# Weighted values: the shared key chunk as two half-column products instead of one full product

## The chip, the cores and the metric

One core of a Trainium2 chip runs the whole program. The metric is the device time in microseconds of one execution. Before the change the median of three runs is 1622.12 us (1620.75 to 1624.53).

## What is computed

Attention that keeps the 32 largest scores of each row, for 8 batches and 8 heads of 576 tokens with 64 features, followed by a gated feed-forward layer over all 4608 tokens. The reference, cut to what matters:

```python
scores = scale * np.matmul(q, k.transpose(0, 1, 3, 2))
kth = np.partition(scores, -top_k, axis=-1)[..., -top_k:-top_k + 1]
scores = np.where(scores >= kth, scores, -1000000000.0)
attn = np.exp(scores - np.max(scores, axis=-1, keepdims=True))
attn = attn / (np.sum(attn, axis=-1, keepdims=True) + 1e-09)
attn_out = np.matmul(attn, v)                      # the change is here
...
gate = 1.0 / (1.0 + np.exp(-(x @ w_gate)))
out = (gate * (x @ w_val)) @ w_out
```

## The kernel before, in words

Heads are worked on in pairs, tokens in tiles of 128 (P), with a last tile of 64 (REM). For each batch, group of tiles and head pair, `run` goes through four stages that overlap over neighbouring steps. `scores` (L219, TensorE) makes the scores of both heads; `select` and `masked` (DVE, ACT, POOL) find each row's threshold and leave the masked exponentials `e`; `turn` (L321, L326, L329) transposes `e` on TensorE so that keys lie on the partitions (`et`, nine chunks of 128 keys, evicted by ACT at L322); `weigh` multiplies by the values.

The nine chunks of `et` hold the keys of two heads laid end to end: chunks 0 to 3 are of the first head, 5 to 8 of the second, and chunk 4 holds the last 64 keys of the first and the first 64 of the second. In `weigh`, for one or two tiles of 128 queries (n = 128 or 256 columns), L340 multiplies a 128x64 block of values of the second head into the upper half of the PSUM tile `po` and L341 one of the first head into the lower half, four times. L342 then multiplies chunk 4 by `mixed`, the blocks 4 and 5 of the value tile side by side (128x128). Block 4 is zero where chunk 4 holds keys of the second head, and block 5 where it holds keys of the first, so one product serves both halves. The last tile of 64 queries goes through L345 to L348, which the change leaves alone.

After the products, L351 transposes `inv`, the inverse row sums, on TensorE into the same PSUM bank (one transpose for each tile of 128 queries); ACT copies it out (`rs`, L354), DVE multiplies (`xf`, L357), ACT and POOL split the result (`xh` L364, `xl` L365), and the feed-forward layer (L396 to L398, L415 to L417, with the weights loaded by L382) consumes it. The value tile comes by one DMA a head pair (L177), with three buffers; `po` has one.

The order of the instructions on each engine isn't written out by hand. The program gives them in the order of `run`, with a rule that holds the feed-forward work behind the attention by a fixed number of tokens (`goal`), and the tile framework's scheduler then sets each engine's order from priorities and its own model of the time (`schedule_with_timeline_sim=True`). So TensorE's instructions from the feed-forward layer, the scores and the transposes are mixed, and a score product can stand in the middle of a `weigh`. All operands of `weigh` are float32, and the hardware makes each float32 product in two passes: every product line shows twice as many matmuls in the trace as the program has. The feed-forward products and the scores of all batches but the first work on a split into two parts (float32r).

Of the kernel before, what the change touches and what calls it, by code (L numbers as in the profile page):

```python
# [28 lines left out]
def tile_topk_attention_then_gated_ffn(  # L29
# [8 lines left out]
    nc = tc.nc  # L38
    P = 128
    B, H, _, S = k.shape  # L40
    D = P // 2
# [290 lines left out]
    def weigh(et, vt, n, invs, pieces, nm):  # L332

        both = ps_o.tile([P, 4 * P], F32, tag="o", name=f"po_{nm}")
        po, rb = both[:, :n], both[:, 2 * P :]
        if n > REM:
            mixed = vt[:, 4:6].rearrange("p a d -> p (a d)")

            for c in reversed(range(4)):
                nc.tensor.matmul(po[D:], vt[:, 6 + c], et[:, 5 + c, :n], start=c == 3, stop=False)  # L340
                nc.tensor.matmul(po[:D], vt[:, c], et[:, c, :n], start=c == 3, stop=False)  # L341
            nc.tensor.matmul(po, mixed, et[:, 4, :n], start=False, stop=True)  # L342
        else:
            for c in range(4):
                nc.tensor.matmul(po[:D], vt[:, c], et[:, c, :REM], start=c == 0, stop=False)  # L345
                nc.tensor.matmul(po[D:], vt[:, 6 + c], et[:, c, REM:P], start=c == 0, stop=False)
            nc.tensor.matmul(po[:D], vt[:REM, 4], et[:REM, 4, :REM], start=False, stop=True)
            nc.tensor.matmul(po[D:], vt[:REM, 10], et[:REM, 4, REM:P], start=False, stop=True)  # L348

        for t, inv in enumerate(invs):  # L350
            nc.tensor.transpose(rb[:, t * P : (t + 1) * P], inv, ident)  # L351
        rs = b2.tile([P, 2 * P], F32, tag="rs", name=f"rs_{nm}")
        m = len(invs) * P
        nc.scalar.activation(rs[:, :m], rb[:, :m], AF.Copy)  # L354
        xf = b2.tile([P, 2 * P], F32, tag="xf", name=f"xf_{nm}")[:, :n]
        if n > REM:
            nc.vector.tensor_tensor(xf, po, rs[:, :n], op=ALU.mult)  # L357
        else:
            for h in range(2):
                d = slice(h * D, h * D + D)  # L360
                nc.vector.tensor_tensor(xf[d], po[d], rs[d, h * REM : h * REM + REM], op=ALU.mult)
        o = 0
        for (xh, xl), c, k in pieces:
            nc.scalar.activation(xh[:, c : c + k], xf[:, o : o + k], AF.Copy)  # L364
            nc.gpsimd.tensor_tensor(xl[:, c : c + k], xf[:, o : o + k], xh[:, c : c + k], op=ALU.subtract)  # L365
            o += k
# [61 lines left out]
    def run(general):  # L428
# [32 lines left out]
        for n in range(len(steps) + 2):  # L461
# [42 lines left out]
            if len(invs) == 2 or i >= end - 1 or i == NT - 1:  # L504

                t, left, pieces = b * S + (i + 1 - len(invs)) * P, o, []
                while left:
                    u, c = t // U, t % U
                    if (u, p) not in xs:
                        if u % 3 == 2 and len(bxs) == 1:  # L510

                            for _ in todo.pop(0) if todo else ():
                                pass
                            split_done()
                        xs[u, p] = [bxs[u % 3 // 2].tile([P, U], F32R, tag=k, name=f"{k}{mark}_{u}_{p}") for k in ("xh", "xl")]
                    k = min(left, U - c)
                    pieces.append((xs[u, p], c, k))
                    t, left = t + k, left - k
                weigh(et, values[g, p], o, invs, pieces, nm)
# [77 lines left out]
```

## Time and profile before

| | |
|---|---|
| median of three runs | 1622.12 us (1620.75 to 1624.53) |
| the profiled execution, its own time | 1619.79 us |
| its span, from the first to the last instruction | 1618.0 us |
| mean granted TensorE clock | 0.981 |
| busy: PE / weight load / DVE / ACT / POOL | 1553.3 / 1391.1 / 1265.3 / 1168.9 / 1206.8 us |

How to read it: PE is TensorE's matmuls, whose shown durations overlap each other because they are pipelined, so the distance between two starts is what one of them takes from its engine. PEld is TensorE's load of the stationary operand, which can run beside the matmul before it. A row `x2` of the timeline merges two neighbours. 1.79 us of the profiled execution's own time lie outside its span.

### The profile page before, as it was taken

The page shows a single profiled execution, that of the slowest core. Times are in us where ns is not written, and L with a number is a line of the kernel's source. Part 1 is how long each engine was busy: PE and PEld are TensorE (multiplying, and loading weights), DVE is VectorE, ACT ScalarE, POOL GpSimd, SP SyncE. Part 2 cuts the span into 40 slices and gives each one's busy share as a digit, 9 for nine tenths or more (in the row PEclk, how much of TensorE's full clock was granted, in tenths as well). Part 3 has the DMA queues.
Part 4 walks back from the last instruction along what each step waited for, and adds up shares of the span by engine and source line. Part 5 has one row for each costly group of instructions (what it writes and reads, how often), then busy time and mean ns, then how long its engine had stood idle before and what let it go on. Part 6 is the DMA issues. An engine that isn't in the chain of part 4 may idle for free.

```text
span 1618.0 us, 33444 instructions
## 1 busy us (share of the span) xinstructions
PE 1553.3 (96%) x10226; PEld 1391.1 (86%) x10226; DVE 1265.3 (78%) x5748; ACT 1168.9 (72%) x2615; POOL 1206.8 (75%) x1923
## 2 busy tenths in 40 slices
PE   5878999899999999999999999999999999999998
PEld 2434897789999999999999999989999999999998
DVE  5999878988888779887888778888788778888300
ACT  6888778977777777777777777777777777777322
POOL 3679977897767896787877886788876996776413
PEclk9878999999999999999999999999999999999999
DMA  7556745665655565565555665655565665554575
GB/s 240 191 187 223 262 166 190 208 217 207 220 191 187 197 247 198 207 227 204 200 193 189 222 234 188 218 175 206 202 200 181 217 225 197 187 200 165 194 268 178
DMA packets 88989, 331.98 MB, mean 205 GB/s; under 512 B 9952, under 2 KB 36576, under 8 KB 61920
## 3 DMA queue, kind: packets, MB, share of 16 engines
q1 hardware_dynamic: 88800, 329.75, 59.0%
q8 instruction: 83, 1.36, 0.3%
q14 instruction: 106, 0.87, 0.2%
HBM read 301.40 MB, written 28.31 MB: 204 GB/s over the span
## 4 chain that ended last, share of the span: by engine, by line
PE 75%; POOL 7%; DVE 4%; ACT 3%; issue 1%; DMA 1%; POOLq 0%; SPq 0%; ACTq 0%
PE pz L396 11%; PE pz L397 11%; PE pz L398 11%; PE pss L219 8%; PE pt L321 6%; PE po L340 6%; PE po L415 5%; PE po L417 5%; PE po L416 5%; POOL u L302 3%; PE po L342 2%; DVE e L238 1%; PE po L351 1%; POOL k L171 1%; DVE kths L310 1%
## 5 line engine op out<-in xcount | busy, mean ns | idle before, releaser
L302 POOL TENSOR_TENSOR u<-s,under 128x288 f32<-128x288 f32 x576 | 444.5, 794 | 83.3 <-ACT under L296 77.3
L284 DVE MAX8 cand<-s 128x8 f32<-128x72 f32 x2304 | 348.1, 218 | 73.4 <-ACT s L226 63.3
L396 PE MATMUL pz<-xh,w 128*128 128x384 f32 x1120 | 383.9, 344 | 0.5 <-ACT gf L401 0.5
L397 PE MATMUL pz<-xl,w 128*128 128x384 f32 x1120 | 380.1, 339 | 0.3 <-POOL xl L365 0.3
L398 PE MATMUL pz<-xh,w 128*128 128x384 f32 x1120 | 379.5, 339 | 0.0
L238 DVE SCALAR_TENSOR_TENSOR e<-s,kths,e 128x576 f32<-128x576 f32 x288 | 291.7, 1020 | 2.8 <-ACT e L233 2.7
L310 DVE MAX8 kths<-u 128x8 f32<-128x584 f32 x288 | 219.6, 763 | 88.5 <-POOL u L303 86.3
L296 ACT ACTIVATE under<-s,leads 128x576 bf16<-128x576 f32 x288 | 223.4, 777 | 43.1 <-DVE leads L288 38.1
L233 ACT ACTIVATE e<-s,st 128x576 f32<-128x576 f32 x288 | 210.1, 774 | 52.0 <-POOL st L292 51.3
L404 POOL TENSOR_TENSOR gl<-gf,gh 128x384 fp32r<-128x384 f32 x144 | 156.0, 1084 | 92.4 <-ACT gh L403 90.3
L322 ACT ACTIVATE et<-pt 128x384 f32<-128x384 f32 x384 | 179.8, 490 | 46.4 <-PE pt L321 45.8
L396 PEld LDWEIGHTS pz<-xh,w 128*128 128x128 f32 x1120 | 210.8, 188 | 1.7 <-ACT gf L401 1.0
L397 PEld LDWEIGHTS pz<-xl,w 128*128 128x128 f32 x1120 | 211.4, 189 | 1.0 <-POOL xl L365 0.6
L398 PEld LDWEIGHTS pz<-xh,w 128*128 128x128 f32 x1120 | 211.1, 189 | 0.0
L226 ACT ACTIVATE s<-pss 128x576 f32<-128x576 f32 x256 | 164.5, 643 | 42.1 <-PE pss L219 41.4
L416 PE MATMUL po<-gl,w 128*128 128x384 f32 x560 | 189.5, 340 | 0.4 <-POOL gl L404 0.3
L415 PE MATMUL po<-gh,w 128*128 128x384 f32 x560 | 188.8, 350 | 0.9 <-ACT acc L419 0.9
L321 PE MATMUL pt<-ident,e 128*128 128x128 f32 x1152 | 184.9, 279 | 4.9 <-DVE e L238 2.6
L417 PE MATMUL po<-gh,w 128*128 128x384 f32 x560 | 187.4, 338 | 0.0
L321 PEld LDWEIGHTS pt<-ident,e 128*128 128x128 f32 x1152 | 144.7, 143 | 28.9 <-DVE e L238 6.5
L219 PE MATMUL pss<-k,qh 128*128 128x288 f32 (+2 forms) x588 | 167.5, 303 | 2.0 <-ACT s L226 2.0
L219 PE MATMUL pss<-k,ql 128*128 128x288 f32 (+2 forms) x588 | 159.1, 293 | 0.0
(105 smaller groups left out, 3318.6 us busy)
## 6 DMA issues: line engine op xcount, KB each, us to landing
w<-ws SPq DMA_DIRECT2D x210, 1024.0 KB, 4.9
v<-in_v_dram SPq DMA_DIRECT2D x64, 352.0 KB, 3.3
wraw<-in_w_dram SPq DMA_DIRECT2D x36, 512.0 KB, 4.4
ws<-wsplit SPq DMA_DIRECT2D x36, 512.0 KB, 3.5
qraw<-in_q_dram SPq DMA_DIRECT2D x140, 128.0 KB, 3.0
kraw<-in_k_dram SPq DMA_DIRECT2D x56, 288.0 KB, 3.8
out_dram<-acc SPq DMA_DIRECT2D x48, 192.0 KB, 4.0
q<-in_q_dram SPq DMA_DIRECT2D x20, 128.0 KB, 3.5
```

What stands on the lines that cost most here:

```text
L219: nc.tensor.matmul(ps[:, half, o : o + n], x[:K, h * P : (h + 1) * P], ks[h][:K, k0 : k0 + n], start=t == 0, stop=t == len(todo) - 1,)
L238: nc.vector.scalar_tensor_tensor(e[:, j], s[:, j], kth[j], e[:, j], op0=ALU.is_ge, op1=ALU.mult, accum_out=st[:, 4 + j : 5 + j])
L284: nc.vector.max(cand[:, j, 8 * g : 8 * g + 8], s[:, j, g * SEG : (g + 1) * SEG])
L302: nc.gpsimd.tensor_tensor(u[:, j, c], s[:, j, c], under[:, j, c], op=ALU.mult)
L310: nc.vector.max(kths[:, at[j] : at[j] + 8], u[:, j])
L321: nc.tensor.transpose(pt[:, c], ef[:, k0 : k0 + P], ident)
L396: nc.tensor.matmul(ps, wt[:, u, 0, d], xh, start=d == 0, stop=False)
L397: nc.tensor.matmul(ps, wt[:, u, 0, d], xl, start=False, stop=False)
L398: nc.tensor.matmul(ps, wt[:, u, 1, d], xh, start=False, stop=d == NP - 1)
L415: nc.tensor.matmul(ps, wt[:, e % 2, 0, f], gh, start=f == 0, stop=False)
L416: nc.tensor.matmul(ps, wt[:, e % 2, 0, f], gl, start=False, stop=False)
L417: nc.tensor.matmul(ps, wt[:, e % 2, 1, f], gh, start=False, stop=f == FG - 1)
```

## The change

In `weigh`, where n > REM, the product of chunk 4 with the 128x128 block `mixed` is replaced by two products of chunk 4 with 128x64 blocks: block 5 into the upper half of `po` and block 4 into the lower half, in the manner of L340 and L341, still last.

```diff
         if n > REM:
-            mixed = vt[:, 4:6].rearrange("p a d -> p (a d)")
-
             for c in reversed(range(4)):
                 nc.tensor.matmul(po[D:], vt[:, 6 + c], et[:, 5 + c, :n], start=c == 3, stop=False)
                 nc.tensor.matmul(po[:D], vt[:, c], et[:, c, :n], start=c == 3, stop=False)
-            nc.tensor.matmul(po, mixed, et[:, 4, :n], start=False, stop=True)
+            nc.tensor.matmul(po[D:], vt[:, 5], et[:, 4, :n], start=False, stop=True)
+            nc.tensor.matmul(po[:D], vt[:, 4], et[:, 4, :n], start=False, stop=True)
```

## Rows read from the trace of the kernel before

**Rows 1.** The page's first part, TensorE's line (busy us, share of the span, instructions), and the first line of its fourth part, the chain of waits that ended last, by engine.

```profile
PE 1553.3 (96%) x10226; PEld 1391.1 (86%) x10226; DVE 1265.3 (78%) x5748; ACT 1168.9 (72%) x2615; POOL 1206.8 (75%) x1923
PE 75%; POOL 7%; DVE 4%; ACT 3%; issue 1%; DMA 1%; POOLq 0%; SPq 0%; ACTq 0%
```

**Rows 2.** Busy time by stage: the stretch, its length, busy us of PE, PEld, DVE, ACT and POOL with the instructions in brackets, the granted TensorE clock, the DMA share and GB/s.

```profile
0.00:265.00 265.00, 219.69 (x1150) 150.47 (x1151) 222.38 (x977) 208.77 (x440) 192.45 (x313) 0.90 0.63 212
265.00:1550.00 1285.00, 1272.36 (x8730) 1180.45 (x8729) 1037.97 (x4763) 945.67 (x2146) 996.83 (x1594) 1.00 0.59 203
```

**Rows 3.** The timeline of TensorE's matmuls (start us, duration us) from the last feed-forward products into one `weigh` of 256 columns: the entry, the first two pairs and the last.

```profile
810.00 0.33 PE L398 MATMUL pz<-xh,w 128*128 128x384 f32 x1
810.17 0.34 PE L396 MATMUL pz<-xh,w 128*128 128x384 f32 x1
810.44 0.43 PE L340 MATMUL po<-et,v 128*64 128x256 f32 x1
810.45 0.43 PE L341 MATMUL po<-et,v 128*64 128x256 f32 x1
810.71 0.38 PE L340 MATMUL po<-et,v 128*64 128x256 f32 x1
...
812.00 0.38 PE L340 MATMUL po<-et,v 128*64 128x256 f32 x1
```

**Rows 4.** The same view at the end of a `weigh` of 256 columns: the first such `weigh` after 265 us, and the last of the span.

```profile
270.09 0.38 PE L340 MATMUL po<-et,v 128*64 128x256 f32 x1
270.41 0.70 PE L342 MATMUL po<-et,v 128*128 128x256 f32 x2
270.94 0.38 PE L351 MATMUL po<-ident,inv 128*128 128x128 f32 x2
271.16 0.49 PE L321 MATMUL pt<-ident,e 128*128 128x128 f32 x3
...
1523.41 0.70 PE L342 MATMUL po<-et,v 128*128 128x256 f32 x2
```

**Rows 5.** The same view at the end of a `weigh` of 128 columns.

```profile
825.36 0.27 PE L340 MATMUL po<-et,v 128*64 128x128 f32 x1
825.46 0.27 PE L340 MATMUL po<-et,v 128*64 128x128 f32 x1
...
825.67 0.49 PE L342 MATMUL po<-et,v 128*128 128x128 f32 x2
826.00 0.27 PE L351 MATMUL po<-ident,inv 128*128 128x128 f32 x1
```

**Rows 6.** The same view where a score product follows a pair of half-column products directly.

```profile
632.67 0.38 PE L340 MATMUL po<-et,v 128*64 128x256 f32 x1
...
632.98 0.40 PE L219 MATMUL pss<-k,qh 128*128 128x288 f32 x1
633.22 0.29 PE L219 MATMUL pss<-k,ql 128*128 128x288 f32 x1
633.35 0.29 PE L219 MATMUL pss<-k,qh 128*128 128x288 f32 x1
```

**Rows 7.** The same view where the transpose of `inv` follows half-column products directly: the end of a `weigh` of the last 64 queries.

```profile
436.82 0.22 PE L348 MATMUL po<-et,v 64*64 64x64 f32 x1
436.97 0.33 PE L351 MATMUL po<-ident,inv 128*128 128x128 f32 x1
437.13 0.71 PE L321 MATMUL pt<-ident,e 128*128 128x128 f32 x5
```

**Rows 8.** Loads of the stationary operand, grouped by line and shape: busy us, mean ns of one, and the idle time of the load queue before them.

```profile
L340 PEld LDWEIGHTS po<-et,v 128*64 128x64 f32 x640 | 77.2, 139 | 43.6 <-issue 10.7 <-ACT et L322 3.0 <-DVE xf L357 2.0
L342 PEld LDWEIGHTS po<-et,v 128*128 128x128 f32 x160 | 23.9, 188 | 23.6 <-issue 23.6
L351 PEld LDWEIGHTS po<-ident,inv 128*128 128x128 f32 x160 | 22.5, 141 | 6.6
```

**Rows 9.** L342 alone by stage: the stretch, its length, busy us of PE and PEld with the passes in brackets.

```profile
0.00:265.00 265.00, 6.73 (x24) 3.60 (x24) 0.90 0.63 212
265.00:1550.00 1285.00, 42.27 (x136) 20.26 (x136) 1.00 0.59 203
```

**Rows 10.** The timeline again, at the two places after 265 us where score products stand between the last pair and L342.

```profile
1255.55 0.30 PE L219 MATMUL pss<-k,ql 128*128 128x288 f32 x1
1255.68 0.38 PE L342 MATMUL po<-et,v 128*128 128x128 f32 x2
...
1405.22 0.40 PE L219 MATMUL pss<-k,qh 128*128 128x288 f32 x1
...
1405.85 0.59 PE L342 MATMUL po<-et,v 128*128 128x256 f32 x2
```

**Rows 11.** The timeline at one place where TensorE stood still twice (in square brackets the idle time before the row, and its releaser).

```profile
1061.23 0.55 PE L321 MATMUL pt<-ident,e 128*128 128x128 f32 x3 [2.16 <-ACT et L322]
1065.95 0.40 PE L219 MATMUL pss<-k,qh 128*128 128x288 f32 x1 [1.80 <-ACT s L226]
```

**Rows 12.** The chain of waits that ended last, in order of time, just ahead of that place.

```profile
1058.69 3.17 DMA v<-in_v_dram
```

**Rows 13.** Busy time by stage, with the columns of rows 2, of the stretch just behind that place.

```profile
1066.60:1069.70 3.10, 3.10 (x12) 3.10 (x11) 3.10 (x12) 1.88 (x5) 2.09 (x4) 0.50 0.61 233
```

**Rows 14.** TensorE's matmuls grouped by line and shape: L342 with 256 columns (passes, busy us, mean ns of one, idle before).

```profile
L342 PE MATMUL po<-et,v 128*128 128x256 f32 x96 | 33.4, 430 | 0.0
```

## The prediction, made before the changed kernel was run

> **What bounds the kernel now.** I read the page's busy times and the chain of waits first. TensorE is busy for 96% of the span and holds 75% of the chain that ended last [rows 1]. Then the stages: up to 265 us TensorE is busy for 219.7 us and waits for the rest; from 265 to 1550 us it is busy for 1272.4 of 1285 us [rows 2]. In that long stage the kernel is as long as TensorE's list of instructions, and 12.6 us of standing still. What the change is worth is therefore read from TensorE's own timeline, by the distances between starts, since the shown durations overlap. 1 us less there is 1 us less in the end, unless a wait takes its place. The sum is made against the profiled execution, 1619.79 us, which is 2.33 us below the median of 1622.12 us. A measurement of this kernel can tell about 0.2% from no change, 3.2 us: faster means below 1618.9 us, slower above 1625.4 us.
>
> **What the timeline shows of a weigh.** L340 and L341 start 0.01 us apart and run together; one such pair of passes takes (812.00 - 810.71) / 6 = 0.215 us at 256 columns [rows 3] and about 0.11 us at 128 [rows 5]. Both ends of a run of half-column products cost something. At the entry, the distance from the last feed-forward product to the first pair is 0.27 us where two of those products are 0.17 apart, and from the first pair to the second it is 0.27 instead of 0.215: 0.10 us for the change of shape and 0.05 us more [rows 3]. From the last pair to L342 there are 0.31 us instead of 0.215, so again 0.10 us. L342's two passes then last from 270.41 to 270.94, 0.53 us, where two passes of 256 columns would be 0.43: another 0.10 us [rows 4]. At 128 columns they last 0.33 us where 0.22 would do, the same 0.11 [rows 5]. The second price doesn't grow with the columns, and it is 0.10 where the new load is 128 columns of values (188 ns, 23.6 us idle on the load queue before it) and 0.05 where it is 64 (139 ns) [rows 8]. I read it as the first load of the stationary operand after the array changes its shape, which can't hide behind an earlier matmul.
>
> **The change part by part.**
> *Removed:* L342, 80 products of two passes each (24 and 136 passes before and after 265 us [rows 9]). At 256 columns: from the last pair's start to L351 270.94 - 270.09 = 0.85 us, and to L321 1.07 us [rows 4]. At 128 columns 0.54 us to L351 [rows 5].
> *Added:* two pairs of passes, 2 x 0.215 = 0.43 us at 256 columns and 0.22 at 128. Two passes of L342 without the switch's price are 0.43 and 0.22 as well, so the streaming is a wash: half-column products that run together stream as fast as one product of the full width.
> *Moved:* the change of shape. It used to fall ahead of L342 and now falls ahead of what comes next on TensorE. The first price, 0.10 us, moves along: a score product that follows a pair directly starts 0.31 us after it [rows 6], as L342 did. The second depends on what comes next. For a score product it is 633.22 - 632.98 = 0.24 instead of 0.13, so 0.11 us [rows 6], and its load is 128 columns of values like L342's: nothing won. For the transpose L351 no run of 128x64 products ends directly in it in this trace. The nearest row is the end of the last 64 queries: there L351 starts 0.15 us after the last pair, and the next transpose 437.13 - 436.97 = 0.16 us after L351, where five transposes in a row stand (0.71 - 0.27) / 4 = 0.11 us apart [rows 7]. So 0.05 us, and the load of L351 is 141 ns, like that of the half-width blocks [rows 8]. The bounds for this price are 0.10 (the shape as such costs it, whatever is loaded) and 0.05; I take 0.05, the row with the same instruction behind the switch.
>
> *The sum.* After 265 us there are 68 such weighs. In 62 of them L351 is the next on TensorE after L342 and a pair directly ahead of it (L342 first at 270.41, last at 1523.41 us [rows 4]): 62 x 0.05 = 3.1 us less. In 4 a score product comes next: 0. In 2 the scheduler put score products between the last pair and L342, which then needs no change of shape [rows 10]; as two half-column products it needs an entry and an exit, 0.10 + 0.05 + 0.10 + 0.05 = 0.30 us each [rows 3, 7]: 0.6 us more. Together 2.5 us less. The 12 weighs before 265 us I cost at nothing: TensorE waits there for other engines, and if that cover were gone it would be 12 x 0.05 = 0.6 us more gain.
>
> *Waits and queues.* No wait is added. The value tile and PSUM tile are released by the same last instructions of the weigh, 0.05 us earlier than before; nothing is moved past the queues of SP or POOL, and L351, for which ACT's copy and the load of the next values wait, stays behind the products. What can change without being in the diff is the order on the engines, since the scheduler places everything by its own times and sees one more product per weigh. So 1619.79 - 2.5 = 1617.3 for the profiled execution, and with the 2.33 us **1619.6 us** for the median, 0.15% less.
>
> **A rule weighed against the rows.** Two starts of one pair lie 0.01 us apart [rows 3], and the 160 starts that are added lie inside the 0.215 us already counted. The Trainium skill's page "TensorEngine Tiling (Array Packing)", section Instruction Overhead, says that each matmul has about 60 cycles of overhead. At the 2.4 GHz level that would be an estimated 25 ns for each of the 160 further passes, 4 us, and the sum would turn to 1.5 us slower; the rows speak against its being additive here.
>
> **The rivals.**
> *No net change.* The second price is 0.10 us whatever the shape change ends in. Then both prices only move, nothing is won, and the two cut weighs cost 0.6 us: 1622.12 + 0.6 = 1622.7 us. For it: both full-width loads of 188 ns show 0.10. Against it: the L351 of rows 7 shows 0.05, though behind 64x64 blocks. The same page's section Key Properties says that changing the tiling mode drains TensorE; by that rule alone the number of drains stays what it was, and the result would be this one.
> *Slower, by more late loads of values.* At 1061 and 1066 us TensorE stands still for 2.16 and 1.80 us [rows 11], just behind a load of values that stands in the chain with 3.17 us [rows 12], and in the 3.1 us behind that its granted clock is 0.50, the 1.2 GHz level [rows 13], where half of the time, 1.5 us, is lost: 5.5 us for one late load. Its place is the load of values, which waits until an earlier weigh lets go of its buffer; it decides once a load lands some 2 us after its products could have started. The order that the scheduler makes anew can have it more often: one more gives 1619.6 + 5.5 = 1625.1, already slower than before, two more 1630.6 us. For it: there are only three buffers. Against it: in the order of before it happens at one place.
> *Faster, by the hitch gone.* The same mechanism the other way: 1619.6 - 5.5 = 1614.1 us. For it: TensorE's 12.6 us of standing still after 265 us are chance products of one order.
> *Far slower, because the pair doesn't overlap.* Both new products stream the same chunk 4, where the pairs of the trace stream different chunks. If that put them one behind the other, each weigh would pay its two pairs twice: with 96 / 2 = 48 weighs of 256 columns [rows 14] and the other 32 of 128, 48 x 0.43 + 32 x 0.22 = 27.7 us, and 1647 us. Nothing in the rows speaks for it.
>
> **How the numbers follow.** The forecast 0.46, with its own range 1617 to 1622 (the early weighs, and some six cuts of a run more or fewer at 0.36 each: exit ahead of a score product 0.21, entry 0.15, from rows 3 and 6); no net change 0.11; one late load more 0.13, two 0.07; the hitch gone 0.19; no overlap 0.04. The predicted time is the forecast's. Of the forecast's 0.46 some 0.19 lies below 1618.9, and of the one late load's 0.13 half above 1625.4. Faster: 0.19 + 0.19 = 0.38. Slower: 0.07 + 0.07 + 0.04 = 0.18. The same: the rest, 0.44. The range, 1612 to 1627 us, takes in one late load more or fewer with most of the forecast's spread around each, and leaves out two late loads and the lost overlap.
>
> **What would show it.** Right: the two new products start 0.01 us apart, two pairs 0.215 us apart at 256 columns; L351 starts 0.31 us after the last pair and the next transpose 0.16 us later; the idle time of the load queue moves from L342 to L351; TensorE's busy time from 265 to 1550 us and its waits stay near 1272 and 12 us. Wrong: 0.21 us from L351 to the next transpose (no net change), new starts 0.2 us apart (no overlap), or waits of 2 us or more for ACT that stand in other places or are gone, in which case the order and not the product set the result.

## The result: slower by 0.74%, and the profile after

The changed kernel takes 1635.81 us (median of four runs, 1633.44 to 1637.23) against 1623.21 us before: ratio 1.0074, 95% interval 1.006 to 1.0088, 12.6 us more. The forecast was 1619.6 us with a range up to 1627.

The page of the changed kernel, TensorE's line and the chain that ended last, to be set against [rows 1]:

```profile
span 1633.9 us, 33795 instructions
PE 1553.7 (95%) x10386; PEld 1378.9 (84%) x10386; DVE 1268.4 (78%) x5748; ACT 1161.4 (71%) x2615; POOL 1210.3 (74%) x1923
PE 61%; DVE 13%; POOL 12%; ACT 7%; issue 3%; DMA 2%; SPq 0%; POOLq 0%; ACTq 0%; DVEq 0%
```

TensorE's busy time is the same (1553.7 us, 1553.3 before). The span grew by 15.9 us in the profiled execution, and that is the time in which TensorE stands still: 1633.9 - 1553.7 = 80.2 us, where it was 1618.0 - 1553.3 = 64.7. The profiled execution of before, at 1619.79 us, was faster than the four that give its median, so about 3 of the 15.9 us are that execution's. The equal busy time is partly chance too: 52.4 us of it before, and 42.9 after, lie in stretches where the granted clock was 0.50. TensorE's share of the chain fell from 75% to 61%; DVE, POOL and ACT took it over. By stage, with the columns of [rows 2]:

```profile
0.00:265.00 265.00, 215.46 (x1166) 143.77 (x1167) 217.40 (x950) 204.42 (x430) 188.55 (x305) 0.90 0.63 206
265.00:1550.00 1285.00, 1261.10 (x8782) 1159.09 (x8781) 1044.31 (x4787) 939.04 (x2149) 999.85 (x1598) 1.00 0.58 201
```

Up to 265 us TensorE is busy for 4.2 us less than before, and from 265 to 1550 us it stands still for 23.9 us instead of 12.6. The waits of TensorE in that second stretch (what waited, for whom; us in total, times, the longest), their head in the changed kernel and then in the kernel before:

```profile
PE pss L219 <- ACT s L226: 5.2, 6, 1.2
PE pz L396 <- POOL xl L364: 2.1, 4, 0.9
PE po L344 <- DVE xf L356: 1.9, 4, 1.0
PE pz L395 <- ACT part L421: 1.9, 1, 1.9
PE wrest L146 <- ACT qh L188: 1.4, 1, 1.4
```

```profile
PE wrest L148 <- POOL wsplit L143: 2.5, 3, 1.2
PE pt L321 <- ACT et L322: 2.2, 1, 2.2
PE pss L219 <- ACT s L226: 2.0, 2, 1.8
```

No long wait was added. There are more short ones, for all three other engines; the longest after 265 us is 1.9 us, and in none of them does TensorE wait for a load of values.

The products themselves do what was forecast. The end of a weigh of 256 columns in the changed kernel, to be set against [rows 4] (here the program has L338 to L341 for the half products and L350 for the transpose):

```profile
412.02 0.38 PE L338 MATMUL po<-et,v 128*64 128x256 f32 x1
412.03 0.38 PE L339 MATMUL po<-et,v 128*64 128x256 f32 x1
412.24 0.38 PE L340 MATMUL po<-et,v 128*64 128x256 f32 x1
412.25 0.38 PE L341 MATMUL po<-et,v 128*64 128x256 f32 x1
412.45 0.38 PE L340 MATMUL po<-et,v 128*64 128x256 f32 x1
412.46 0.38 PE L341 MATMUL po<-et,v 128*64 128x256 f32 x1
412.77 0.44 PE L350 MATMUL po<-ident,inv 128*128 128x128 f32 x2
```

The new products start within 0.01 us of each other, two pairs are 0.21 us apart, and L350 starts 0.31 us after the last. Its two transposes last 0.44 us together where L351's last 0.38 in [rows 4]. One alone lasts 0.27 [rows 5], so the second starts 0.17 us after the first, where it was 0.11 (0.16 to 0.17 at all 40 such places after 265 us): the price behind the switch is 0.05 to 0.06 us, and the 0.21 us that would have meant no net change are not there. The load queue's idle time, with the columns of [rows 8], moved from L342 (23.6 us) to L350:

```profile
L340 PEld LDWEIGHTS po<-et,v 128*64 128x64 f32 x160 | 21.0, 139 | 7.2 <-issue 0.9
L350 PEld LDWEIGHTS po<-ident,inv 128*128 128x128 f32 x160 | 18.9, 140 | 25.1 <-issue 21.1 <-POOL k L171 0.4 <-POOL st L241 0.4
```

What differs everywhere is the order. The trace has 10226 matmuls of TensorE before and 10386 after. Laid side by side in order of time, without line and buffer numbers, at least 4450 of them must be taken out or put in to turn the one list into the other, where the change alone would take 480 (160 passes out, 320 in). The first new products stand where the full one stood, and right behind them a transpose of `e` has been put off. The theory is that this order, not the products, costs the 12.6 us; the rival, that the half products cost it themselves.

### The profile page after: what moved, and what is told of

The parts are those of the page before. It is cut to its first block, busy times and chain, and to the rows that moved or that the text cites. A ratio compares the mean times of both kernels' runs of the same rounds, so it can differ in the third digit from the quotient of the medians.

```text
span 1633.9 us, 33795 instructions
## 1 busy us (share of the span) xinstructions
PE 1553.7 (95%) x10386; PEld 1378.9 (84%) x10386; DVE 1268.4 (78%) x5748; ACT 1161.4 (71%) x2615; POOL 1210.3 (74%) x1923
## 4 chain that ended last, share of the span: by engine, by line
PE 61%; DVE 13%; POOL 12%; ACT 7%; issue 3%; DMA 2%; SPq 0%; POOLq 0%; ACTq 0%; DVEq 0%
PE pz L395 9%; PE pz L396 9%; PE pz L397 9%; PE pss L219 6%; PE pt L321 5%; PE po L414 5%; POOL u L302 4%; PE po L338 4%; PE po L415 4%; PE po L416 4%; DVE e L238 3%; DVE kths L310 3%; DVE cand L284 3%; ACT e L233 2%; POOL acc L422 2%
## 5 line engine op out<-in xcount | busy, mean ns | idle before, releaser
L322 ACT ACTIVATE et<-pt 128x384 f32<-128x384 f32 x384 | 181.7, 491 | 37.7 <-PE pt L321 37.2
```

## The experiments

**How an order was held.** In these kernels the program is traced twice. A scratch program, never run, is scheduled; the order of each engine's instructions is read from it; then the program that runs is traced, and each instruction is tied to the one ahead of it on its engine by an edge without a semaphore (shortened, with the names of one of the runs):

```python
order = build("full")[2]                 # scratch: the order of every engine
nc, arrays, found = build("halves", order)
...                                      # inside build, where an order is given:
for x, y in zip(chain, chain[1:]):       # chain: one engine's instructions in that order
    tc.add_manual_dep(insts[y], x, mybir.DependencyInfo(
        mybir.DependencyClass.NoSync, mybir.DependencyReason.DATA), reason="order of the other kernel")
```

With the half products in the old order, the trace's list of TensorE differs from that of the kernel before in exactly those 480 matmuls, and the lists of DVE, ACT, POOL and of the DMA issues in nothing.

**Products of the change, order of before.** 

> The two half-column products of the change, but every engine issues its instructions in the order of the kernel before (the full product replaced in place by the two). Order theory (the loss comes from the new order that the scheduler made, and the products are as the prediction costed them): 2 to 3 us faster than before, 1620 to 1621 us, TensorE idle after 265 us near 12.6 us as before. Product theory (the half products themselves cost the 12.6 us, by the way they run or by what waits for them): about 1635 us.

Measured: 1621.98 us, ratio 0.9995 (0.9987 to 1.0004). The loss is gone. The two timelines hold the same instructions in the same order, so they can be laid over each other matmul by matmul. In the 62 weighs where a transpose comes next after 265 us, the time from the last matmul ahead of the weigh's products to the first behind its transposes shrank by 0.047 us at 256 columns (41 weighs) and 0.050 at 128 (21), by the median; in the two where score products stand in between it grew by 0.296 and 0.299. All 68 together: about 2.4 us less. The second of those two in this kernel (L342, L343 are the loop's products here, L345, L346 the new ones, L359 the transpose), against [rows 10]:

```profile
1408.63 0.29 PE L221 MATMUL pss<-k,ql 128*128 128x288 f32 x1
1408.86 0.43 PE L345 MATMUL po<-et,v 128*64 128x256 f32 x1
1408.87 0.43 PE L346 MATMUL po<-et,v 128*64 128x256 f32 x1
1409.13 0.38 PE L345 MATMUL po<-et,v 128*64 128x256 f32 x1
1409.13 0.38 PE L346 MATMUL po<-et,v 128*64 128x256 f32 x1
1409.44 0.44 PE L359 MATMUL po<-ident,inv 128*128 128x128 f32 x2
```

The entry costs 0.23 instead of 0.13 and 0.27 instead of 0.215 us, the exit 0.31. Of the 2.4 us about 0.8 (none to 2.1 by the interval) arrive at the end. In the profiled execution TensorE's busy time fell to 1549.9 us and it stood still for 71.0 us instead of 64.7, but this execution took 1622.72 us and that of before 1619.79, so how much of the gain went into waits is not shown.

**Product of before, order of the change.** 

> The full 128x128 product of the kernel before, but every engine issues in the order of the changed kernel (where score products stand between the two halves, the full product takes the place of the second). Order theory: as slow as the changed kernel or slower by the 2 to 3 us that the half products save, 1636 to 1639 us, TensorE idle after 265 us near 24 us. Product theory: about 1623 us.

Measured: 1634.37 us, ratio 1.0073 (1.0061 to 1.0085): the whole loss without a single half product. It lies under the expected 1636 to 1639 us: the half products, which were to be 2 to 3 us faster in the same order, took 1635.81, so their gain does not show at the end here either. From 400 to 1600 us TensorE's busy time, in the kernel before, in the changed one, and here:

```profile
400.00:1600.00 1200.00, 1194.49 (x8201) 1118.31 (x8199) 922.37 (x4262) 848.31 (x1929) 893.01 (x1424) 1.00 0.59 205
```

```profile
400.00:1600.00 1200.00, 1188.26 (x8287) 1104.36 (x8287) 933.40 (x4282) 843.14 (x1933) 895.66 (x1428) 1.00 0.58 203
```

```profile
400.00:1600.00 1200.00, 1189.35 (x8167) 1109.48 (x8166) 933.09 (x4282) 841.11 (x1932) 894.85 (x1428) 1.00 0.58 203
```

It stands still for 5.5, 11.7 and 10.7 us: the longer waits come with the order. Up to 400 us it is busy for 347.6, 338.3 and 336.5 us.

**Another order for each product.** Only the distance of the feed-forward work is changed:

```diff
-    BEHIND = 480
+    BEHIND = 490
```

The full product: 

> The kernel before with the feed-forward work held back by 490 tokens instead of 480: the same work, another order from the scheduler. If the order alone moves the time by chance: anywhere in 1613 to 1637 us. If the order of before is nothing special: within 3 us of 1623.

Measured: 1613.88 us, ratio 0.9946 (0.9932 to 0.996). The half products: 

> The changed kernel with 490 instead of 480 tokens, to be set against full_behind490. If the half products lead the scheduler to a worse order as a rule: 10 to 14 us slower than full_behind490. If it was the chance of one order: within 6 us of it, with either sign.

Measured: 1621.28 us, 0.9987 (0.9978 to 0.9996), 7.4 us slower than the full product at the same distance, which lies between the two expectations (within 6, or 10 to 14 us). Twice the half products had the worse order, so the next runs asked whether that is a rule.

**Does the scheduler's belief in a longer weigh spoil the order?** The full product ran in orders taken from two scratch programs, written out here by what their weighs have in its place:

```diff
-            nc.tensor.matmul(po, mixed, et[:, 4, :n], start=False, stop=True)
+            nc.tensor.matmul(po[:, : n // 4], mixed, et[:, 4, : n // 4], start=False, stop=True)   # short
...
+            nc.tensor.matmul(po[D:], vt[:, 5], et[:, 4, :n], start=False, stop=True)               # three: a third half, behind the two of the change
```

> The work of the kernel before (full product), with every engine's order taken from a scratch program, never run, in which the full product has only a quarter of its columns, so that the scheduler counts a shorter weigh. Bias theory (the order gets worse the longer the scheduler believes the weigh to be): at or below 1623 us, about 1615 to 1620. Chance theory (each order is a draw, whatever the scheduler believes): anywhere in 1613 to 1637 us.

Measured: 1616.47 us, 0.996 (0.9947 to 0.9973).

> The work of the kernel before, with every engine's order taken from a scratch program with a third half-column product in each weigh, so that the scheduler counts a still longer weigh than in the changed kernel. Bias theory: slower than the full product in the changed kernel's order, above 1634 us, about 1640 to 1650. Chance theory: anywhere in 1613 to 1637 us, as likely below 1634 as above.

Measured: 1630.89 us, 1.0053 (1.0033 to 1.0074): slow, but not slower than the order with two halves. The first is what the bias theory expected; the second is not, since it wanted more than 1634 us. Both lie in the wide range of the chance theory, which they could hardly have missed.

**The distance the other way.** `BEHIND = 470`. 

> The kernel before with the feed-forward work held back by 470 tokens instead of 480. Chance theory: anywhere in 1613 to 1637 us. If the distance itself sets the time (490 gave 1613.9, 480 gives 1622.7): about 1630.

Measured: 1631.23 us, 1.0055 (1.0037 to 1.0073). 

> The changed kernel with 470 instead of 480 tokens, to be set against full_behind470. Bias theory: slower than it by 7 to 13 us, as at 490 and 480. Chance theory: the difference may have either sign, within 15 us.

Measured: 1621.7 us, 0.999 (0.9981 to 1.0). Here the half products are 9.5 us faster than the full one. The differences at 470, 480 and 490 are -9.5, +12.6 and +7.4 us, so a worse order is no rule for the half products; a bias of a few us can't be excluded with three pairs. For the full product alone the third expectation came true: its time falls as the distance grows (1631.2, 1622.7, 1613.9 us). That of the half products doesn't (1621.7, 1635.8, 1621.3), so the distance isn't the whole of it, but that it helps the full product can't be excluded.

**Both at their best.** The half products at 490 in the order that the full product got there. 

> The two half products of the change, with 490 tokens, every engine in the order that the scheduler made for the full product with 490 tokens (full_behind490, 1613.9 us). Order theory: as fast as that kernel or up to 2.5 us faster, 1611 to 1614 us, and so faster than both the kernel before and the changed one. If the half products cost something that the old order hid: 1616 us or more.

Measured: 1612.17 us, 0.9939 (0.9927 to 0.9951): 0.6% faster than the kernel before, and faster than the changed one. With products and distance alike, the order that the scheduler made for the half products took 1621.28 us: 9.1 us for the order alone. Against the full product in that order (0.9946) the gain of the products is again at most a few tenths of a per cent, within the noise.

**Where in the program the order loses.** One order up to a cut after the first fifth of the traced instructions, the other behind it, on every engine, with the full product. 

> The work of the kernel before. The instructions of the first fifth of the program stand in the changed kernel's order, the others in the order before. If the time is lost where the lag of the changed kernel first grows (11 of its 16 us by 300 us of the span): 1630 to 1634 us. If an early lag is made up by TensorE later, and the loss is spread over the whole: 1623 to 1626.

Measured: 1645.07 us, 1.0145 (1.0128 to 1.0162). 

> The counterpart: the first fifth in the order before, the rest in the changed kernel's. If the loss is made early: 1623 to 1627 us. If it is spread over the whole: 1632 to 1634.

Measured: 1647.25 us, 1.015 (1.0133 to 1.0167). Neither expectation was met: both are slower than either whole order. One row of TensorE's waits in the one and in the other:

```profile
PE pz L404 <- DMA w<-ws: 18.4, 1, 18.4
```

```profile
PE pz L404 <- DMA w<-ws: 18.3, 1, 18.3
```

TensorE waits 18 us for a load of weights, once, between 265 and 420 us, which neither whole order does: a wait that the cut brings with it. So the times don't place the loss. The stretch behind the cut can still be read: from 400 to 1600 us TensorE stands still for 5.3 us with the old order there and for 12.6 us with the new one.

```profile
400.00:1600.00 1200.00, 1194.70 (x8232) 1118.23 (x8231) 942.35 (x4355) 858.73 (x1954) 903.05 (x1445) 1.00 0.59 205
```

```profile
400.00:1600.00 1200.00, 1187.37 (x8184) 1105.99 (x8183) 944.95 (x4325) 847.52 (x1946) 897.40 (x1443) 1.00 0.58 203
```

So 6 to 7 us of the loss are made there, as in the changed kernel (11.7 against 5.5 us), and the rest ahead of it: up to 400 us TensorE was 9.3 us behind in busy time.

**The full product in six orders.** The median time and, from one profiled execution each, TensorE's busy time and its standing still, in us:

| order | time | busy | standing still |
|---|---|---|---|
| distance 490 | 1613.88 | 1546.5 | 65.5 |
| from the short scratch program | 1616.47 | 1547.0 | 66.2 |
| before | 1622.7 | 1553.3 | 64.7 |
| from the scratch program with three halves | 1630.89 | 1550.3 | 78.7 |
| distance 470 | 1631.23 | 1548.1 | 78.8 |
| of the changed kernel | 1634.37 | 1550.6 | 81.1 |

The three slow orders stand still for 14 to 16 us longer than the order of before. The two fast ones stand still for as long as it does, and are faster because TensorE is busy for 6 to 7 us less over the same matmuls. In the short program's order 38.7 us of the busy time lie in stretches with a granted clock of 0.50, against 52.4 before; at half the clock half of that time is lost, so by this estimate the difference is worth 6.9 us, all of that gain. At 490 it is 48.0 us, worth 2.2 of the 6.8; the rest is not explained.

## Why the prediction was wrong

- *What bounds the kernel*: right in that TensorE is the busiest engine before and after (96% and 95% of the span). "1 us less there is 1 us less in the end" is not borne out: of 2.4 us at most 2.1 arrived with the order held, and in that stage TensorE already waited for all three other engines now and then.
- *The cost of the products*: right, to the tenth. The streaming is a wash, the change of shape moved to what comes next, and costs 0.05 us ahead of a transpose where it cost 0.10 ahead of L342; the two cut weighs cost 0.30 each. The sum of 2.5 us less is 2.4 on the timeline of the run with the order held. The 160 further passes lie inside 0.215 us a pair. The Trainium skill's page "TensorEngine Tiling (Array Packing)", section Instruction Overhead, gives each matmul about 60 cycles of overhead; as a cost added to the streaming it does not show in these rows.
- *No net change* as a rival: its mechanism was wrong (the price did fall to 0.05), though the time with the order held is near it (0.7 us under before, where the rival had 0.6 above and the forecast 2.5 under).
- *Waits and queues*, the step that failed. It named the scheduler's new order as what can change without standing in the diff, and then took the order of before as the likeliest outcome and one late load of values, 5.5 us, as the size of a surprise. "No wait is added" failed with it: 23.9 us of standing still after 265 us, not 12.6. The runs show that one more product in 80 places gives a new order from the first weigh on, and that this order alone costs the loss: the old product in it takes 1634.4 us, the new products in the old order 1622.0. The sign that the prediction names for this is there: the waits of 2.16 and 1.80 us for ACT are gone. The same full product spreads over 20 us in six orders, 18 us in the four at distance 480, against 2.4 us for what was computed with care.
- *Slower, by more late loads of values*: the sign was right by luck, the mechanism wrong. TensorE waits for no load of values after 265 us in the changed kernel; it has more short waits for ACT, POOL and DVE. Even the hitch of [rows 11] was no such wait. The load of [rows 12] landed at 1061.86 us, when TensorE had been running again since 1061.23. TensorE had waited for ACT to copy out `et` (L322), and ACT, ahead of that, for POOL:

```profile
1059.37 1.44 ACT L233 ACTIVATE e<-s,st 128x576 f32<-128x576 f32 x2 [1.06 <-POOL st L292]
1060.71 0.47 ACT L322 ACTIVATE et<-pt 128x384 f32<-128x384 f32 x1
```

- The range, 1612 to 1627 us, was too narrow for a new order. Even the spread seen since (9 us below to 12 us above the order of before), laid around the forecast, ends at 1631 us, below the measured time.

What of an order makes it good is open: the runs tie the time to the order, not to one feature of it.

## What to carry to other kernels

Where a scheduler sets the order, a change of a few instructions has two effects: its own cost, which the timeline can give in advance (here to a tenth of a microsecond), and a new order, which here was worth several times more. Hold the order of the old kernel to measure the first, and try several orders (another distance, the order of another program) before a change is kept or thrown away for the second. Here two half-width products that run together streamed as fast as one full product, and leaving their shape ahead of a transpose was 0.05 us cheaper than ahead of a full product of values.

## What the runs showed of the hardware

A change of the array's shape between 128x128 and 128x64 products showed two prices that add. The first was 0.10 us at every place read: into the half-width products (0.27 instead of 0.17 us behind feed-forward products, 0.23 instead of 0.13 behind score products) and out of them (0.31 instead of 0.215). The second came one matmul later: 0.05 us where a 64-column block or a transpose follows (loads of 139 and 140 ns), and 0.10 to 0.11 us where 128 columns of values or keys do (188 and 189 ns). The trace of before suggested this; the changed kernel, where the 128x64 products end in a transpose, has the 0.05. That the load is the reason is a reading of these rows, since no run varied the load alone.
